# Side jobs of a backward pass in another order, and one filled region dealt unevenly over the DMA engines

## The chip, the cores and the metric

The kernel runs on one core of a Trainium2 chip, in one launch. The metric is the device time of that launch in microseconds (us). Five engines take part: PE (matmul), DVE (vector), ACT (scalar), POOL (GpSimd) and SP (sync). SP and POOL here mostly issue DMAs; all DMAs run on the same 16 DMA engines.

## The reference

One decoder block for a single token, forward and backward, with the gradients of all inputs as outputs. Cut to what matters:

```python
# x: 1x1x448; caches: 8 heads x 32768 x 256; window W = 4096 last positions
def A(x, k_cache, v_cache, wq, wo):
    q = (x @ wq) as 16 heads of 256          # two query heads per cache head
    k, v = last W rows of the caches
    p = softmax(q k^T / 16); o = p v
    return o @ wo
def B(x, w_gate, w_up, w_down):
    return ((x @ w_gate) * (x @ w_up)) @ w_down
h  = x + A(layernorm(x), k_cache, v_cache, wq, wo)
h2 = h + B(layernorm(h), w_gate, w_up, w_down)
out, vjp = jax.vjp(h2 as a function of x, caches, wq, wo, w_gate, w_up, w_down)
return out, *vjp(grad_out)
```

The outputs are out_0 (the block's output), out_1 (gradient of x), out_2 and out_3 (gradients of the K and V caches), out_4 to out_8 (gradients of wq, wo, w_gate, w_up, w_down). The cache gradients have the caches' full shape, 8 x 32768 x 256 in bf16. Only the last 4096 rows of each head depend on anything; the other 28672 rows are zeros and must be written too. That is 14 MB for each of 16 regions (8 heads, two caches), and most of what the kernel moves.

## The kernel before

**Zeros.** A tile `zeros` of 128 x 8192 bf16 is set by one DVE memset. Then SP issues 16 DMAs (line 58), one per head and cache, in the order out_2, out_3 of head 0, then of head 1 and so on. Each writes one region as 896 rows of 16 KB, so 56 rows for each of the 16 DMA engines. SP does nothing else. This is called the fill, and its queue the fill queue; in the profile it is the hardware queue q1.

**Everything else on POOL.** All other transfers are issued by POOL, through the software queue q0: first the rows x and grad_out (lines 88 and 90), then wq (line 92), then the K and V windows, 2 MB each, through eight slots of a tile `S`. POOL issues in program order, so a DMA that waits for something holds back those behind it. Where the program text doesn't force an order, a scheduler chose how the instructions of one engine are interleaved.

**Forward.** For each cache head g: scores, softmax, and moments (lines 308 to 335). Then wo, w_gate and w_up are loaded, the second half of the block is computed, and the gradient comes back to `dh_bc`, `doT` and `dq_bc` (lines 380 to 463).

**Backward, eight stages.** The loop at line 546 has one stage for each cache head g. A stage transposes the head's V window on PE (line 554), forms `dp` (line 559), and builds 32 blocks of the two cache gradients in PSUM (line 588). ACT and DVE in turn copy them (`evac`, lines 208 to 213) into two slots of `S`. The slots alternate by `STG = [5, 6, 7, 0]`, so stage g needs the slots from which stage g-2 was written out. At its end the stage issues two DMAs of 2 MB (line 593, the copy-outs). Three V windows no longer fit and are loaded again during stages 1 to 3 (line 563).

**Side jobs.** After the copy-outs of stage g the text calls the jobs in `side[g]` (line 594). They make the gradients of the weights and the two rows:

- `outer` (line 472) scales a broadcast row on DVE into one of two buffers in `Mt` (`stage_buf`, alternating) and issues the buffer as one DMA. A job must wait until the DMA of two jobs before has landed. o4 to o8 are the five weight gradients.
- `ffn_out` (line 490) loads w_down into the tile `Rt`, makes the block's output row with 14 matmuls and 14 small ones, and writes out_0.
- `dxn_part(i0, i1)` (line 507) loads a part of wq again into `Rt`, and reduces it against `dq_bc` on DVE (line 510). Both parts use the same place in `Rt`. `dx_out` then writes out_1.

Of the kernel before, what the change touches and what calls it, by code (L numbers as in the profile page):

```python
# [7 lines left out]
bf16 = mybir.dt.bfloat16  # L8
# [5 lines left out]
D = 448  # L14
NI = 7
H = 16
G = 8
Dh = 256
W = 4096
# [3 lines left out]
Sk = 32768  # L23
# [5 lines left out]
HQ = H * Dh // 2  # L29
HF = F // 2  # L30
ZW = 8192
# [9 lines left out]
def kernel(  # L41
# [4 lines left out]
    FILL = nc.sync  # L46
    IO = nc.gpsimd

    const = ctx.enter_context(tc.tile_pool(name="const", bufs=1))
    small = ctx.enter_context(tc.tile_pool(name="small", bufs=2))  # L50
    ps = ctx.enter_context(tc.tile_pool(name="ps", bufs=1, space=bass.MemoryType.PSUM))

    zeros = const.tile([128, ZW], bf16)
    V_.memset(zeros[:], 0.0)
    for g in range(G):
        for o in (out_2, out_3):
            reg = o[0, g, 0:Sk - W, :].rearrange("s d -> (s d)").rearrange("(p n f) -> p n f", p=128, f=ZW)
            FILL.dma_start(out=reg, in_=zeros[:].unsqueeze(1).to_broadcast([128, NZ, ZW]))


    S = const.tile([128, NS, SLOT], bf16)
# [21 lines left out]
    def flat_rows(w):  # L83
        return w.rearrange("a b -> (a b)").rearrange("(p x) -> p x", p=128)


    x_bf = const.tile([1, D], bf16, tag="rowa", name="x_bf")
    IO.dma_start(out=x_bf[:], in_=A_x.rearrange("a b d -> (a b) d"))
    go_bf = const.tile([1, D], bf16, tag="rowb", name="go_bf")
    IO.dma_start(out=go_bf[:], in_=grad_out.rearrange("a b d -> (a b) d"))  # L90
    wq_sb = S[:, 1:3, :].rearrange("p a b -> p (a b)")[:, 0:NI * HQ]
    IO.dma_start(out=wq_sb, in_=flat_rows(A_wq))
    load_K(0)
# [58 lines left out]
    def half_to_row(dst, z, bcast, first=True):  # L152

        d3 = dst.rearrange("o (m r) -> o m r", r=NI)
        n = 0
        for i in range(NI):
            for s in range(2):
                lt = z[:, i:i + 1].to_broadcast([128, 128]) if bcast else z[:, i:i + 1]
                P_.matmul(d3[:, :, (7 * s + i) // 2], lhsT=lt, rhs=ident_f[:, s::2],  # L159
                          start=(first and n == 0), stop=(n == 2 * NI - 1), skip_group_check=True)  # L160
                n += 1
# [6 lines left out]
    def layernorm(X, tag):  # L168
        s1 = small.tile([128, 1], f32, tag="ln_s")
        V_.reduce_sum(out=s1[:], in_=X, axis=AX)  # L170
        nm = small.tile([128, 1], f32, tag="ln_nm")
        V_.tensor_scalar(out=nm[:], in0=total(s1[:], 1)[:], scalar1=-1.0 / (2 * D), scalar2=None, op0=ALU.mult)
        xc = small.tile([128, NI], f32, tag="ln_xc")
        V_.tensor_scalar(out=xc[:], in0=X, scalar1=nm[:, 0:1], scalar2=None, op0=ALU.add)
        sq = small.tile([128, NI], f32, tag="ln_sq")
        s2 = small.tile([128, 1], f32, tag="ln_s2")
        V_.tensor_tensor_reduce(out=sq[:], in0=xc[:], in1=xc[:], scale=1.0, scalar=0.0, op0=ALU.mult, op1=ALU.add, accum_out=s2[:])
        rstd = const.tile([128, 1], f32, tag=tag + "rstd")
        S_.activation(out=rstd[:], in_=total(s2[:], 1)[:], func=ACT.Sqrt, bias=eps_t[:, 0:1], scale=1.0 / (2 * D))
        V_.reciprocal(out=rstd[:], in_=rstd[:])  # L180
        xh = const.tile([128, NI], f32, tag=tag + "xh")
        V_.tensor_scalar(out=xh[:], in0=xc[:], scalar1=rstd[:, 0:1], scalar2=None, op0=ALU.mult)
        xb = const.tile([128, NI], bf16, tag=tag + "xb")
        V_.tensor_copy(out=xb[:], in_=xh[:])
        xf = const.tile([128, NI], f32, tag=tag + "xf")
        V_.tensor_copy(out=xf[:], in_=xb[:])
        xx = const.tile([128, NI, 2], bf16, tag=tag + "xx")
        V_.tensor_tensor(out=xx[:], in0=xf[:].unsqueeze(2).to_broadcast([128, NI, 2]), in1=msk[:], op=ALU.mult)
        return rstd, xh, xf, xx
# [30 lines left out]
    rstd1, xh1, xf1, xx1 = layernorm(xX[:], "ln1")  # L220
# [21 lines left out]
    oT_f = const.tile([128, 32], f32)  # L242
    oT_bf = const.tile([128, 32], bf16)
    kbar = const.tile([128, 32], f32)
    dh2_bc = const.tile([128, D], bf16)
# [96 lines left out]
    bc2 = [S[:, 7, NI * HF:NI * HF + F].rearrange("p (i c) -> p i c", i=2), Rt[:, NI * HF:NI * HF + F].rearrange("p (i c) -> p i c", i=2)]  # L342
# [43 lines left out]
    rstd2, xh2, xf2, xx2 = layernorm(hX[:], "ln2")  # L386
# [44 lines left out]
    dh_bc = const.tile([128, D], bf16)  # L431
# [30 lines left out]
    dq_bc = late[:, 0:2 * HQ].rearrange("p (i c) -> p i c", i=2)  # L462
# [4 lines left out]
    def stage_buf():  # L467
        k = 1 + st_ctr[0] % 2
        st_ctr[0] += 1
        return late[:, k * 4096:(k + 1) * 4096]  # L470

    def outer(dst, n0, n1, src, scal, width):

        sb = stage_buf()[:, 0:(n1 - n0) * width].rearrange("p (n c) -> p n c", c=width)
        for n in range(n0, n1):
            V_.tensor_scalar(out=sb[:, n - n0, :], in0=src(n), scalar1=scal[:, n:n + 1], scalar2=None, op0=ALU.mult)
        IO.dma_start(out=dst[:, n0:n1, :], in_=sb)

    o4 = flat_rows(out_4).rearrange("p (i c) -> p i c", i=NI)
    o5 = out_5.rearrange("(b p) n -> p b n", p=128)  # L480
    o6 = flat_rows(out_6).rearrange("p (i c) -> p i c", i=NI)
    o7 = flat_rows(out_7).rearrange("p (i c) -> p i c", i=NI)
    o8 = out_8.rearrange("(c p) n -> p c n", p=128)

    hh = const.tile([128, FC], f32)
# [4 lines left out]
    def ffn_out():  # L490
        wd1 = Rt[:, 0:FC * D].rearrange("p (c n) -> p c n", n=D)
        IO.dma_start(out=wd1, in_=B_w_down.rearrange("(c p) n -> p c n", p=128))
        hX2 = small.tile([128, NI], f32, tag="hX2")
        V_.tensor_scalar(out=hX2[:], in0=hX[:], scalar1=0.5, scalar2=None, op0=ALU.mult)
        t = ps.tile([1, D], f32, tag="tmp", bufs=1)
        for c in range(FC):
            P_.matmul(t[:], lhsT=hh_bf[:, c:c + 1], rhs=wd1[:, c, :], start=(c == 0), stop=False, skip_group_check=True)
        half_to_row(t[:], hX2[:], False, first=False)
        h2 = const.tile([1, D], bf16, tag="rowb", name="h2")
        V_.tensor_copy(out=h2[:], in_=t[:])  # L500
        IO.dma_start(out=out_0.rearrange("a b d -> (a b) d"), in_=h2[:])

    Pq = const.tile([128, NI], f32)
    wq2 = Rt[:, 0:4 * HQ].rearrange("p (i c) -> p i c", c=HQ)
    wq_d = flat_rows(A_wq).rearrange("p (i c) -> p i c", i=NI)

    def dxn_part(i0, i1):
        IO.dma_start(out=wq2[:, 0:i1 - i0, :], in_=wq_d[:, i0:i1, :])
        for i in range(i0, i1):
            V_.tensor_tensor_reduce(out=wq2[:, i - i0, :], in0=wq2[:, i - i0, :], in1=dq_bc[:, i % 2, :], scale=1.0, scalar=0.0,  # L510
                                    op0=ALU.mult, op1=ALU.add, accum_out=Pq[:, i:i + 1])

    def dx_out():
# [4 lines left out]
        V_.tensor_copy(out=dx[:], in_=t[:])  # L518
        IO.dma_start(out=out_1.rearrange("a b d -> (a b) d"), in_=dx[:])

    side = {
        0: [lambda: outer(o6, 0, 4, lambda i: bc2[0][:, i % 2, :], xf2, HF), lambda: outer(o6, 4, 7, lambda i: bc2[0][:, i % 2, :], xf2, HF),
            lambda: outer(o7, 0, 4, lambda i: bc2[1][:, i % 2, :], xf2, HF), lambda: outer(o7, 4, 7, lambda i: bc2[1][:, i % 2, :], xf2, HF)],
        1: [ffn_out] + [lambda b=b: outer(o5, b, b + 8, lambda n: dh_bc[:], oT_f, D) for b in (0, 8)],
        2: [lambda b=b: outer(o5, b, b + 8, lambda n: dh_bc[:], oT_f, D) for b in (16, 24)],
        3: [lambda b=b: outer(o8, b, b + 7, lambda n: dh2_bc[:], hh, D) for b in (0, 7)],
        4: [lambda: dxn_part(0, 4)],
        5: [lambda: dxn_part(4, 7), dx_out],
        6: [lambda i=i: outer(o4, i, min(i + 2, 7), lambda n: dq_bc[:, n % 2, :], xf1, HQ) for i in (0, 2)],
        7: [lambda i=i: outer(o4, i, min(i + 2, 7), lambda n: dq_bc[:, n % 2, :], xf1, HQ) for i in (4, 6)],  # L530
    }


    STG = [5, 6, 7, 0]
# [3 lines left out]
    rowb = late[:, 14336:16384].rearrange("p (k a c) -> p k a c", k=2, a=8)  # L538
# [7 lines left out]
    for g in range(G):  # L546
# [24 lines left out]
        rows = rowb[:, g % 2]  # L571
# [11 lines left out]
        for c in range(T // 2):  # L583
            d_ps = bps.tile([128, 2, 2, Dh], f32, tag="d2", bufs=2)
            for i in range(2):
                t = 2 * c + i
                k, a = t // 8, t % 8
# [38 lines left out]
```

## Time and profile before

| | us |
|---|---|
| median of 3 runs | 818.56 (818.16 to 818.86) |
| the profiled execution, its own time | 818.39 |
| its span, from first to last instruction | 816.6 |
| PE / DVE / ACT busy | 497.6 / 376.8 / 164.9 |

338.66 MB move in this span, at a mean of 415 GB/s. The page's slices are 1/40 of the span each; "DMA" there is the mean busy share of the 16 engines in tenths. In answers about windows the share stands as a number (1.00 is all engines busy), and GB/s beside it. In answers about order of time, the columns are start, duration, engine, line, operation, tiles, count, and in brackets the idle time of that engine just before and what ended it. A DMA's completion adds one count for each of the 16 engines, and the trace holds the time of each count; sorted, these sixteen times tell how far apart the engines are, though not which engine is which.

### The profile page before, as it was taken

What the parts mean: (1) busy time and instruction counts of PE and PEld (TensorE: products, weight loads), DVE (VectorE), ACT (ScalarE), POOL (GpSimd) and SP (SyncE); (2) the same over time, 40 slices, a digit from 0 to 9 for tenths busy, and PEclk for the clock granted to TensorE, in tenths of its full rate; (3) what the DMA queues carried; (4) which work ended last, traced back from release to release, by engine and by line L of the source; (5) the groups of instructions that cost most, each with busy time, mean ns of one, the idle gap of its engine ahead of it and who ended that gap; (6) DMA issues with size and microseconds to landing.
All of it is one profiled execution on the core that took longest, in us unless ns stands there. A gap on an engine that the chain in (4) does not pass through costs nothing.

```text
span 816.6 us, 12117 instructions
## 1 busy us (share of the span) xinstructions
PE 497.6 (61%) x4947; PEld 300.9 (37%) x4991; DVE 376.8 (46%) x1149; ACT 164.9 (20%) x261; POOL 41.7 (5%) x77
## 2 busy tenths in 40 slices
PE   3558869999574946062993468799378940001770
PEld 3545646666343523031981332345124410001110
DVE  4127847667461643028732354565255440404550
ACT  0220201221101000000011233355244420000440
POOL 4000000000000001000000000010010000000000
PEclk9959888999695969565555556555555555555555
DMA  8999999999999999999999999999999999999985
GB/s 322 431 424 429 427 429 426 429 427 426 432 423 426 424 420 418 427 429 432 423 430 427 417 413 426 428 402 429 419 404 426 423 428 400 424 415 432 431 355 237
DMA packets 24632, 338.66 MB, mean 415 GB/s; under 512 B 1312, under 2 KB 1376, under 8 KB 4736
## 3 DMA queue, kind: packets, MB, share of 16 engines
q1 hardware_dynamic: 14592, 234.88, 68.2%
q0 software_dynamic: 9984, 103.00, 30.2%
q8 instruction: 39, 0.64, 0.3%
q14 instruction: 17, 0.14, 0.0%
HBM read 57.28 MB, written 280.59 MB: 414 GB/s over the span
## 4 chain that ended last, share of the span: by engine, by line
issue 50%; DMA 22%; PE 14%; another core or an unknown queue 4%; DVE 4%; POOL 2%; ACT 1%; POOLq 0%; DVEq 0%; ACTq 0%
DMA out_dram<-Mt 9%; DMA out_dram<-S 5%; DMA S<-in_A_wo_dram 4%; PE dq_ps L453 3%; PE d_ps L588 3%; PE tr L554 2%; DMA S<-in_A_v_cache_dram 2%; DMA S<-in_A_wq_dram 2%; PE MT L322 2%; DVE Rt L423 1%; DVE Rt L510 1%; POOL S L75 1%; PE dh_ps L159 1%; DVE S L212 1%
## 5 line engine op out<-in xcount | busy, mean ns | idle before, releaser
L322 PE MATMUL MT<-Rt,S 128*128 128x512 bf16 x468 | 146.7, 391 | 22.5 <-DMA S<-in_A_v_cache_dram 19.8
L588 PE MATMUL d_ps<-R,Mt 32*128 32x512 bf16 x256 | 121.1, 605 | 58.6 <-DVE S L212 57.9
L318 DVE TENSOR_SCALAR Rt<-S,pf 128x256 bf16<-128x256 bf16 x512 | 118.0, 282 | 31.6 <-PE acc L329 16.5
L212 DVE CAST S<-d_ps 128x512 bf16<-128x512 f32 x128 | 87.1, 689 | 63.4 <-ACT S L210 55.6
L210 ACT CAST S<-d_ps 128x512 bf16<-128x512 f32 x128 | 74.9, 586 | 127.7 <-PE d_ps L588 127.7
L266 PE MATMUL tr<-ident_bf,S 128*128 128x128 bf16 x512 | 51.5, 264 | 43.4 <-DMA S<-in_A_k_cache_dram 40.1
L325 PEld LDWEIGHTS <-S 128*128 128x128 bf16 x512 | 50.1, 99 | 62.9 <-issue 7.2
L554 PE MATMUL tr<-ident_bf,S 128*128 128x128 bf16 x512 | 67.6, 304 | 0.7 <-ACT Mt L210 0.7
L588 PEld LDWEIGHTS <-Mt 32*128 32x128 bf16 x256 | 22.8, 113 | 112.8 <-issue 110.8
L329 PE MATMUL acc<-ones_bf,Rt 128*128 128x1 bf16 x1024 | 62.0, 164 | 0.0
L554 PEld LDWEIGHTS <-S 128*128 128x128 bf16 x512 | 48.4, 136 | 24.4 <-issue 24.4
L266 PEld LDWEIGHTS <-S 128*128 128x128 bf16 x512 | 40.5, 120 | 41.9 <-DMA S<-in_A_k_cache_dram 40.6
L325 PE MATMUL acc<-pT_all,S 128*128 128x2 bf16 x512 | 49.3, 166 | 2.6 <-issue 0.9
L165 PE MATMUL t<-st,ones_f 128*128 128x2 f32 x4 | 1.2, 364 | 79.6 <-DVE st L196 79.6
L210 ACT COPY Rt<-tr 128x1024 bf16<-128x1024 bf16 x32 | 32.4, 1012 | 85.1 <-PE tr L266 84.6
L210 ACT COPY Mt<-tr 128x1024 bf16<-128x1024 bf16 x32 | 32.4, 1014 | 60.8 <-PE tr L554 34.3
L329 PEld LDWEIGHTS <-Rt 128*128 128x128 bf16 x1024 | 44.5, 96 | 0.0
L212 DVE COPY Rt<-tr 128x1024 bf16<-128x1024 bf16 x32 | 22.1, 689 | 47.5 <-PE tr L266 46.2
L322 PEld LDWEIGHTS <-S 128*128 128x128 bf16 x512 | 32.2, 97 | 22.3 <-DMA S<-in_A_v_cache_dram 20.0
L331 ACT COPY Mt<-MT 128x512 f32<-128x512 f32 x8 | 4.7, 586 | 165.1 <-remote 73.8
L510 DVE CUSTOM_DVE_ANT_0 Rt<-Rt,Mt 128x2048 bf16<-128x2048 bf16 x7 | 15.6, 2289 | 48.3 <-DMA Rt<-in_A_wq_dram 48.3
L212 DVE COPY Mt<-tr 128x1024 bf16<-128x1024 bf16 x32 | 22.0, 686 | 22.9 <-PE tr L554 15.5
(184 smaller groups left out, 463.5 us busy)
## 6 DMA issues: line engine op xcount, KB each, us to landing
out_dram<-zeros SPq DMA_DIRECT2D x16, 14336.0 KB, 155.7
out_dram<-S POOLq DMA_DIRECT2D x16, 2048.0 KB, 31.0
S<-in_A_v_cache_dram POOLq DMA_DIRECT2D x11, 2048.0 KB, 35.6
S<-in_A_k_cache_dram POOLq DMA_DIRECT2D x8, 2048.0 KB, 27.9
out_dram<-Mt POOLq DMA_DIRECT2D x6, 896.0 KB, 18.2
S<-in_A_wq_dram POOLq DMA_DIRECT2D x1, 3584.0 KB, 15.3
S<-in_A_wo_dram POOLq DMA_DIRECT2D x2, 1792.0 KB, 35.6
out_dram<-Mt POOLq DMA_DIRECT2D x3, 1024.0 KB, 32.5
```

The source lines that it names most:

```text
L75: IO.dma_start(out=dst, in_=cache[0, g, Sk - W:, :].rearrange("(p t) d -> p t d", t=T))
L210: S_.copy(out=out, in_=in_)
L212: V_.tensor_copy(out=out, in_=in_)
L266: P_.transpose(tr[:, i, dh, :], Xw[:, 4 * q + i, dh * 128:(dh + 1) * 128], ident_bf[:])
L318: V_.tensor_scalar(out=pk[:, i, h, :], in0=K[:, t, :], scalar1=pf[:, t, h:h + 1], scalar2=None, op0=ALU.mult)
L322: P_.matmul(MT[:, hf, :], lhsT=Vv[:, t, hf * 128:(hf + 1) * 128], rhs=pk[:, i, :, :].rearrange("p h d -> p (h d)"), start=(t == 0), stop=( ...
L325: P_.matmul(acc[:, 2 * hf:2 * hf + 2], lhsT=Vv[:, t, hf * 128:(hf + 1) * 128], rhs=pT_all[:, g, t, :], start=(t == 0 and hf == 0), stop=(t ...
L329: P_.matmul(acc[:, 4 + 2 * h + dk:5 + 2 * h + dk], lhsT=pk[:, i, h, dk * 128:(dk + 1) * 128], rhs=ones_bf[:, 0:1], start=False, stop=(t == ...
L453: P_.matmul(dq_ps[:, 2 * h + dk:2 * h + dk + 1], lhsT=Mt[:, h // 2, hf, c0:c0 + 128], rhs=doT_f[:, 2 * h + hf:2 * h + hf + 1], start=(hf = ...
L510: V_.tensor_tensor_reduce(out=wq2[:, i - i0, :], in0=wq2[:, i - i0, :], in1=dq_bc[:, i % 2, :], scale=1.0, scalar=0.0, op0=ALU.mult, op1=A ...
L554: P_.transpose(tr[:, i, dh, :], Vw[g][:, 4 * q + i, dh * 128:(dh + 1) * 128], ident_bf[:])
L588: P_.matmul(d_ps[:, i, :, :].rearrange("p w d -> p (w d)"), lhsT=rows[32 * k:32 * k + 32, a, :], rhs=R[32 * k:32 * k + 32, :], start=True, ...
```

## The change

1. The loads of the rows x and grad_out go from POOL to SP, ahead of the fill.
2. The last fill region (out_3, head 7) is written by three DMAs in place of one. Its 896 rows of 16 KB are dealt as 640 rows over 16 engines, 16 rows in pieces of 2 KB over 16 engines, and 240 rows in pieces of 8 KB with an outermost dimension of 15. If the last runs on 15 engines, 15 engines write 57 rows of the region and one writes 41.
3. `dxn_part` loses its load, which becomes `dxn_load`. `ffn_out`, the two o7 jobs and the first wq reload are called ahead of the stages. The two wq parts and `dx_out` move from stages 4 and 5 to stages 0 and 1; o5 moves from stages 1 and 2 to 2 and 3, o8 from 3 to 4, o4 from 6 and 7 to 5 and 6. Stage 7 has no job.

```diff
+    x_bf = const.tile([1, D], bf16, tag="rowa", name="x_bf")
+    FILL.dma_start(out=x_bf[:], in_=A_x.rearrange("a b d -> (a b) d"))
+    go_bf = const.tile([1, D], bf16, tag="rowb", name="go_bf")
+    FILL.dma_start(out=go_bf[:], in_=grad_out.rearrange("a b d -> (a b) d"))
     zeros = const.tile([128, ZW], bf16)
...
+            if g == G - 1 and o is out_3:
+                break
             FILL.dma_start(out=reg, in_=zeros[:].unsqueeze(1).to_broadcast([128, NZ, ZW]))
+    rows = out_3[0, G - 1, 0:Sk - W, :].rearrange("s d -> (s d)").rearrange("(r f) -> r f", f=ZW)
+    FILL.dma_start(out=rows[0:640].rearrange("(p n) f -> p n f", p=128), in_=zeros[:].unsqueeze(1).to_broadcast([128, 5, ZW]))
+    FILL.dma_start(out=rows[640:656].rearrange("r (a c) -> (r a) c", a=8), in_=zeros[:, 0:ZW // 8])
+    FILL.dma_start(out=rows[656:896].rearrange("(e n) (a f) -> e (n a) f", e=15, a=2),
+                   in_=zeros[0:127:9, 0:ZW // 2].unsqueeze(1).to_broadcast([15, 32, ZW // 2]))
...
-    x_bf = const.tile([1, D], bf16, tag="rowa", name="x_bf")
-    IO.dma_start(out=x_bf[:], in_=A_x.rearrange("a b d -> (a b) d"))
-    go_bf = const.tile([1, D], bf16, tag="rowb", name="go_bf")
-    IO.dma_start(out=go_bf[:], in_=grad_out.rearrange("a b d -> (a b) d"))
...
+    def dxn_load(i0, i1):
+        IO.dma_start(out=wq2[:, 0:i1 - i0, :], in_=wq_d[:, i0:i1, :])
+
     def dxn_part(i0, i1):
-        IO.dma_start(out=wq2[:, 0:i1 - i0, :], in_=wq_d[:, i0:i1, :])
...
     side = {
-        0: [o6 0:4, o6 4:7, o7 0:4, o7 4:7],        # each an outer(...), shortened here
-        1: [ffn_out, o5 0:8, o5 8:16],
-        2: [o5 16:24, o5 24:32],
-        3: [o8 0:7, o8 7:14],
-        4: [dxn_part(0, 4)],
-        5: [dxn_part(4, 7), dx_out],
-        6: [o4 0:2, o4 2:4],
-        7: [o4 4:6, o4 6:7],
+        0: [o6 0:4, o6 4:7, dxn_part(0, 4), dxn_load(4, 7)],
+        1: [dxn_part(4, 7), dx_out],
+        2: [o5 0:8, o5 8:16],
+        3: [o5 16:24, o5 24:32],
+        4: [o8 0:7, o8 7:14],
+        5: [o4 0:2, o4 2:4],
+        6: [o4 4:6, o4 6:7],
+        7: [],
     }
+    ffn_out()
+    o7 0:4, o7 4:7
+    dxn_load(0, 4)
```

As the scheduler now deals the instructions out, POOL issues after the loads of the forward pass: w_down, a part of o7, a part of o6, out_0, the rest of o7, the first wq part, the rest of o6, a part of o5, a V window, the second wq part, and only then the copy-outs of stage 0. The last of the o4 jobs stands on DVE within the copies of stage 7, and its DMA on POOL between the copy-outs of stages 6 and 7.

More of the change, by code (lines that the diff above doesn't have):

```diff
@@ L519, in dx_out, with o4_job, o5_job, o67_job @@
         IO.dma_start(out=out_1.rearrange("a b d -> (a b) d"), in_=dx[:])
-    side = {
[L522 to L530, printed above, removed]
-    }
+    def o4_job(i):
+        return lambda: outer(o4, i, min(i + 2, 7), lambda n: dq_bc[:, n % 2, :], xf1, HQ)
+    def o5_job(b):
+        return lambda: outer(o5, b, b + 8, lambda n: dh_bc[:], oT_f, D)
+    def o67_job(w, i0, i1):
+        return lambda: outer((o6, o7)[w], i0, i1, lambda i: bc2[w][:, i % 2, :], xf2, HF)
+    side = {
+        0: [o67_job(0, 0, 4), o67_job(0, 4, 7), lambda: dxn_part(0, 4), lambda: dxn_load(4, 7)],
+        1: [lambda: dxn_part(4, 7), dx_out],
+        2: [o5_job(0), o5_job(8)],
+        3: [o5_job(16), o5_job(24)],
+        4: [lambda b=b: outer(o8, b, b + 7, lambda n: dh2_bc[:], hh, D) for b in (0, 7)],
+        5: [o4_job(0), o4_job(2)],
+        6: [o4_job(4), o4_job(6)],
+        7: [],
+    }
+    ffn_out()
+    o67_job(1, 0, 4)()
+    o67_job(1, 4, 7)()
+    dxn_load(0, 4)
     STG = [5, 6, 7, 0]
```

## Prediction

> **What bounds the kernel now.** I read the page first (DMA by slice, then by queue), then the windows at the end, the timelines of POOL and DVE, and the completion counts of the last DMAs.
>
> ```profile
> DMA  8999999999999999999999999999999999999985
> q1 hardware_dynamic: 14592, 234.88, 68.2%
> q0 software_dynamic: 9984, 103.00, 30.2%
> ```
>
> The DMA engines are busy from the first slice to the last but two, and the fill (q1) is two thirds of that. So an engine's wait elsewhere costs nothing as long as each DMA engine has packets of one queue or the other. What can be won is at the two ends, and in how evenly the 16 engines finish.
>
> ```profile
> 1.31 0.62 POOL L88 DMA_DIRECT2D x_bf<-in_A_x_dram  x1 [0.85 <-POOLq L610]
> 1.93 0.50 POOL L90 DMA_DIRECT2D go_bf<-in_grad_out_dram  x1
> 2.42 0.55 POOL L92 DMA_DIRECT2D S<-in_A_wq_dram  x1
> ```
>
> At the start the first large transfer, wq, is issued behind the two small rows, at 2.42.
>
> ```profile
> 765.00:778.00 13.00, 9.73 (x22) 2.09 (x21) 7.72 (x12) 6.43 (x11) 0.00 (x0) 0.50 1.00 427
> 785.00:790.00 5.00, 3.78 (x9) 0.86 (x9) 2.77 (x4) 2.42 (x5) 0.00 (x0) 0.50 0.97 415
> 790.00:795.00 5.00, 3.83 (x9) 0.90 (x9) 2.77 (x4) 2.40 (x5) 0.00 (x0) 0.50 0.54 229
> 795.00:800.00 5.00, 1.76 (x4) 0.24 (x2) 2.08 (x3) 1.17 (x2) 1.06 (x2) 0.50 0.49 206
> 800.00:805.00 5.00, 0.00 (x0) 0.00 (x0) 0.00 (x0) 0.00 (x0) 0.00 (x0) 0.50 1.00 423
> 805.00:810.00 5.00, 0.00 (x0) 0.00 (x0) 0.00 (x0) 0.00 (x0) 0.00 (x0) 0.50 0.80 341
> ```
>
> The last two numbers are the DMA share and GB/s. Half of the engines idle from 790 to 800, then the last copy-outs run alone. Why those are late:
>
> ```profile
> 675.01 0.69 DVE L212 CAST S<-d_ps 128x512 bf16<-128x512 f32 x1 [0.17 <-ACT S L210]
> 700.63 2.29 DVE L510 CUSTOM_DVE_ANT_0 Rt<-Rt,Mt 128x2048 bf16<-128x2048 bf16 x1 [24.94 <-DMA Rt<-in_A_wq_dram]
> 732.93 2.29 DVE L510 CUSTOM_DVE_ANT_0 Rt<-Rt,Mt 128x2048 bf16<-128x2048 bf16 x1 [23.36 <-DMA Rt<-in_A_wq_dram]
> ...
> 642.91 0.53 POOL L508 DMA_DIRECT2D Rt<-in_A_wq_dram  x1
> 707.65 0.53 POOL L508 DMA_DIRECT2D Rt<-in_A_wq_dram  x1 [31.13 <-DVE Pq L510]
> 778.77 0.54 POOL L593 DMA_DIRECT2D out_dram<-S  x1 [0.17 <-issue]
> 797.73 0.53 POOL L593 DMA_DIRECT2D out_dram<-S  x1 [18.42 <-ACT S L210]
> 798.45 0.53 POOL L593 DMA_DIRECT2D out_dram<-S  x1 [0.19 <-issue]
> ```
>
> DVE sits twice for a wq reload queued behind copy-outs (24.94 and 23.36 us), and the copies of stages 6 and 7 sit behind it on DVE. Stages 0 to 5 issued their copy-outs at 504, 537, 570, 605, 642 and 675, some 34 us apart; those of 6 and 7 come at 778 and 798.
>
> Now the engines. Completion counts in the trace, sorted, of the last fill DMA and of the last copy-out:
>
> ```
> fill, issued 639.96:     777.9 778.1 781.6 781.9 782.0 782.2 782.2 782.5 782.8 785.2 792.4 792.9 797.5 798.3 803.4 805.5
> copy-out, issued 798.45: 809.1 809.1 809.2 809.2 809.2 809.2 809.2 809.2 809.4 809.4 809.5 809.5 810.2 810.5 813.1 814.6
> ```
>
> The slowest engine is still filling at 805.5, when the last copy-out has long been queued: it never idles, and its 814.6 is simply all its work. One engine is late all along (the fill DMA issued at 303.87 ends at 439.7 on it and by 430.3 on the other 15; that of 392.72 at 536.0 against 521.1). The other late ones fell back between 676 and 733, where GB/s drop to 404 and 413. Most engines are different: their second-last pair of copy-outs lands by about 792, the last two (8 packets of 0.611 us each, 4.9 us a DMA) run from 799.4 to 809.2, and 7.5 us in between are idle.
>
> **The change, part by part.** I work against the profiled execution: last landing 814.6, plus 2.0 to the end of the span (816.6), plus 1.8 outside it (818.39). The median, 818.56, is 0.2 above that.
>
> *Start.* wq moves up by the two issues before it, 2.42 - 1.31 = 1.1 us, and with it all later DMA work: -1.1. Bounds: 0 (the rows' reader is no earlier, since DVE's memset runs to 5.14 and the rows landed at 3.1 and 3.6) and -1.6 (both issues and the gap before them). SP issues the two rows in the time in which it waited 5.1 us for the memset; cost nil, and at most 1.1 on the fill, which has wq's packets beside it until its own first packet at 9.65.
>
> *Last fill region.* A 16 KB fill packet takes 0.611 us. 56 of them: 34.2 us per engine. New, on 15 engines: 40 x 0.611 = 24.4; 8 packets of 2 KB, between the rows of 1792 B (0.078) and 2688 B (0.107), taken at 0.085: 0.7; 32 packets of 8 KB at 0.309 (the o4 rows): 9.9. Sum 35.0, +0.8. On the spared engine 25.1, -9.1. Two more SP issues (0.6 us each unless the queue is full) lie under fill already queued.
>
> [...]
>
> *Which engine is late.* The counts show one engine that is late throughout. [...]
>
> *Side jobs.* Bytes and packets stay the same, only their place moves. Per part:
> - The seven reductions of line 510 (2.29 us each, 16 us of DVE) and their two loads leave stage 6's front and enter the copies of stages 0 and 1. Gone: 24.94 + 23.36 of DVE waiting. Added: the first part is issued near 445 and queues behind 7 us of o7, so it lands by about 470, when stage 0's copies start at 475: hidden. The second waits on POOL for the fourth reduction (about 497) and lands some 13 us later; DVE waits for it ahead of the last three copies of stage 0, and behind it on POOL stand the copy-outs of stage 0. Those go from 503.6 to about 520: 9 us of reductions and 7 of waiting.
> - `ffn_out`'s matmuls (14 x 0.58 plus 28 small ones, about 10 us of PE) move from 494-506 to the stretch near 424-440, where PE waited 7.0 once. At worst 10 us more: stage 0 by 520 to 530.
> - o7 ahead of o6 uses the same bytes. o5, o8 and o4 go one stage on; two of them a stage queue 20 us (896-byte rows: 8 blocks are 10 us), beside 20 us of copy-outs, so 34 us a stage rises to at most 40 in stages 2 to 4 and falls after.
> - The last o4 job waits on DVE within stage 7 for its buffer; behind it stand five eighths of stage 7's copies. That buffer's DMA was issued two jobs earlier, with at most 35 us of queue before it, about a stage ago: hidden; 0 to 10 us if not.
>
> So stage 7 issues its last copy-outs at 520 + 7 x 34 = 758 to 530 + 7 x 36 = 782, in place of 798. The fill outlives them and no engine runs dry: the most common engine then has all its work done by 809.2 - 7.5 - 1.1 + 0.8 = 801.4. Cover lasts until 791, about 10 us before that (two copy-outs alone).
>
> *The sum.* What counts is the engine with most work. Spared, if it is the late one: 814.6 - 1.1 - 9.1 = 804.4. The next: 813.1 - 1.1 + 0.8 = 812.8, if the late stretch of 676 to 733 returns as it was. The mean over all engines of (landing minus idle) is 804.8; with the start and the uneven deal 803.9: the floor, if all end together. Between floor and 812.8 I have no row, since that lateness fell in the windows of the wq reloads and those go elsewhere, to times with less in the software queue. I take half of the lateness over 801.4, that is 5.7: last landing 807.1. Span 809.1, time 810.9, by 7.5 us (0.9%) faster.
>
> **The rivals.**
> - *The others stay as late.* For it: engines without idle never catch up. Against: the slow stretches go with transfers that move. 812.8 + 3.8 = 816.6, a gain of 0.2%.
> - *The wrong engine is spared.* Nothing in the profile says which engine the 15 leave out. The late one then keeps its 16 rows and gets another: 814.3 + 3.8 = 818.1, no change. The reordering alone brings nothing, since the slowest engine had no idle time to lose.
> - *Stage 7 comes later, slower than before.* The place: DVE in stages 2 to 6, in order, with copies behind a `Mt` buffer whose DMA stands behind copy-outs (lines like 5.96 and 5.39 us of waiting before line 476 at 656 and 666). The last copy-out takes 10.7 us from issue to landing on a free engine, so it decides from an issue at 791 on and costs time against before from about 805: seven stages of 40.7 us in place of 34. At 42 us a stage the issue is at 814 and the time about 829.
>
> **How the numbers follow.** Differences under 0.2% (1.6 us) can't be told from no change here. The forecast case 0.64, all of it faster; others stay as late 0.14, split 0.08 faster and 0.06 same; wrong engine 0.10 (0.09 same, 0.01 slower); late stage 7 0.12 (0.01 same, 0.11 slower). Faster 0.72, same 0.16, slower 0.12. The range: the floor is 803.9 + 3.8 = 807.7, less what the slow stretches might cost less at their new place (404 and 413 GB/s in place of 429, over 24 and 25 us, are 1.4 and 0.9 us an engine, of which I count three quarters, 1.7), so 806.0; upwards through both "as late" and "wrong engine" to 818.5. Outside lie the late stage 7 and a little below, together under 0.2.
>
> **What would show it.** Right: wq issued near 1.3; no wait of 20 us before line 519 (the old 510); the last copy-outs issued by 785; DMA share 1.00 until about 800; the last completion counts of the fill, not of a copy-out, at the end, within some 6 us of each other. Wrong: one engine's count over 8 us behind the rest (wrong engine), or a window of DMA share near 0.5 ahead of the last copy-outs (late stage 7).

## Result, and the profile after

The changed kernel takes 826.96 us (median; 826.53 to 827.41) against 818.56 before: a ratio of 1.0087, 95% interval 1.006 to 1.0114 (intervals below, in brackets, are of the same kind). It is about 1% slower, where 810.9 was predicted, 0.9% faster. Its profiled execution has a span of 825.1 us and a time of 826.87. The other runs below were each taken beside new runs of the kernel before, whose medians are 818.71 to 819.23 and whose single runs go up to 825.7; a difference is taken against those beside it where nothing else is said.

The page of the changed kernel, DMA by slice, GB/s by slice, and the two large queues:

```profile
DMA  8999999999999999999999999999999999999981
GB/s 343 429 424 430 430 429 426 427 427 429 427 424 428 413 425 420 426 431 431 423 430 428 411 419 430 431 419 425 410 429 427 420 416 421 423 423 428 425 326 37
...
q1 hardware_dynamic: 14979, 234.88, 67.5%
q0 software_dynamic: 9920, 103.00, 29.9%
```

The megabytes are those of before. The last slice carried 237 GB/s before and carries 37 now: for some 20 us almost nothing moves, and yet the kernel has not ended. The side jobs did what they were moved for. POOL's and DVE's timelines (start, duration, engine, line, and in brackets the idle time before with its releaser):

```profile
1.29 0.67 POOL L99 DMA_DIRECT2D S<-in_A_wq_dram  x1 [0.83 <-POOLq L631]
...
513.88 2.29 DVE L519 CUSTOM_DVE_ANT_0 Rt<-Rt,Mt 128x2048 bf16<-128x2048 bf16 x1 [20.18 <-DMA Rt<-in_A_wq_dram]
...
518.76 0.54 POOL L614 DMA_DIRECT2D out_dram<-S  x1 [34.15 <-ACT S L217]
520.62 0.54 POOL L614 DMA_DIRECT2D out_dram<-S  x1 [1.33 <-DVE S L219]
...
762.22 0.53 POOL L614 DMA_DIRECT2D out_dram<-S  x1 [16.40 <-ACT S L217]
762.95 0.53 POOL L614 DMA_DIRECT2D out_dram<-S  x1 [0.19 <-issue]
```

wq goes out at 1.29, stage 0's copy-outs at 519 and 521, the last ones at 762 and 763, 35 us earlier than before. All compute is over by then. The end of the windows (the last two numbers are DMA share and GB/s):

```profile
760.00:780.00 20.00, 1.01 (x2) 0.10 (x1) 1.58 (x3) 0.91 (x2) 1.06 (x2) 0.50 1.00 424
...
785.00:790.00 5.00, 0.00 (x0) 0.00 (x0) 0.00 (x0) 0.00 (x0) 0.00 (x0) 0.50 0.99 399
790.00:795.00 5.00, 0.00 (x0) 0.00 (x0) 0.00 (x0) 0.00 (x0) 0.00 (x0) 0.50 0.93 355
795.00:800.00 5.00, 0.00 (x0) 0.00 (x0) 0.00 (x0) 0.00 (x0) 0.00 (x0) 0.50 0.93 348
800.00:805.00 5.00, 0.00 (x0) 0.00 (x0) 0.00 (x0) 0.00 (x0) 0.00 (x0) 0.50 0.44 159
805.00:810.00 5.00, 0.00 (x0) 0.00 (x0) 0.00 (x0) 0.00 (x0) 0.00 (x0) 0.50 0.25 77
810.00:815.00 5.00, 0.00 (x0) 0.00 (x0) 0.00 (x0) 0.00 (x0) 0.00 (x0) 0.50 0.06 21
...
820.00:825.00 5.00, 0.00 (x0) 0.00 (x0) 0.00 (x0) 0.00 (x0) 0.00 (x0) 0.50 0.04 18
```

Two things are to be read here. From 810 on the share is 0.06, one engine of sixteen (1/16 = 0.0625): one engine ends alone. And from 790 to 800 the share stays at 0.93 while GB/s fall from 424 to 350: engines are busy and move less. The half-idle stretch of before (share 0.49 to 0.54 from 790 to 800) is gone. The completion counts of the three DMAs of the last region, sorted, say the same:

```
640 rows, issued 639.39 (its last three counts): 797.8 798.5 813.2
16 rows in 2 KB, issued 693.91:             784.9 786.0 790.4 790.9 791.0 791.0 791.1 791.5 791.8 792.6 792.7 794.3 796.4 798.8 799.9 814.1
15 pieces, issued 714.40:   747.5 | 800.4 800.7 800.7 800.7 800.8 800.8 801.6 802.4 802.5 803.9 807.7 808.6 809.7 811.5 823.9
```

The third DMA has one count at 747.5, long before its data can have moved and just after SP ended its issue (714.40 + 32.66 = 747.06), and fifteen behind it: it runs on 15 engines. The late engine is one of the fifteen. It ends its packets of 2 KB at 814.1 and then writes 32 packets of 8 KB alone, 9.8 us, until 823.9. The wrong engine was spared.

That explains 0.8 us (one more row of 16 KB on this engine), not 10. The rest is in the packets' durations. Between 797 and 811 the late engine's 16 KB packets take up to 1.27 us in place of 0.611, while one other engine's 8 KB packets take 0.60 to 0.645 in place of 0.309, in step with them. Some of both, with their starts and durations in the trace:

```
late engine, 16 KB:     803.09 1.272   804.37 1.272   805.65 1.272   806.93 1.272   808.20 1.255
another engine, 8 KB:   803.41 0.644   804.06 0.638   804.71 0.644   805.36 0.638   806.01 0.645
```

Both move at half speed; the eleven packets of the late engine from 797 to 810.7 cost it 7 us. In the whole trace 43 of the 480 packets of 8 KB are over 0.5 us.

### The profile page after: what moved, and what is told of

Read it like the earlier page. It is cut to its first block, busy times and chain, and to the rows that moved or that the text cites. A ratio compares the mean times of both kernels' runs of the same rounds, so it can differ in the third digit from the quotient of the medians.

```text
span 825.1 us, 12157 instructions
## 1 busy us (share of the span) xinstructions
PE 508.6 (62%) x4991; PEld 304.1 (37%) x4991; DVE 374.7 (45%) x1149; ACT 165.0 (20%) x261; POOL 40.4 (5%) x75
## 4 chain that ended last, share of the span: by engine, by line
issue 58%; DMA 16%; PE 11%; DVE 4%; POOL 3%; ACT 1%; POOLq 0%; DVEq 0%
DMA S<-in_A_wo_dram 4%; DMA Rt<-in_A_wq_dram 4%; DMA out_dram<-Mt 3%; PE dq_ps L460 3%; DMA S<-in_A_k_cache_dram 3%; DMA S<-in_A_v_cache_dram 2%; PE MT L329 2%; POOL out_dram L484 1%; POOL S L86 1%; DVE Rt L430 1%; POOL out_dram L614 1%; PE dh_ps L166 1%; PE ao L390 1%; PE d_ps L609 1%; PE tr L575 1%
## 5 line engine op out<-in xcount | busy, mean ns | idle before, releaser
L609 PE MATMUL d_ps<-R,Mt 32*128 32x512 bf16 x256 | 124.4, 612 | 92.5 <-DVE S L219 91.8
L329 PE MATMUL MT<-Rt,S 128*128 128x512 bf16 x512 | 157.7, 392 | 20.3 <-DMA S<-in_A_v_cache_dram 19.4
L273 PE MATMUL tr<-ident_bf,S 128*128 128x128 bf16 x512 | 54.1, 273 | 44.2 <-DMA S<-in_A_k_cache_dram 41.0
L332 PEld LDWEIGHTS <-S 128*128 128x128 bf16 x512 | 50.0, 99 | 63.1 <-issue 7.2
L575 PE MATMUL tr<-ident_bf,S 128*128 128x128 bf16 x512 | 68.8, 304 | 3.5 <-ACT Mt L217 3.5
L575 PEld LDWEIGHTS <-S 128*128 128x128 bf16 x512 | 48.5, 135 | 28.0 <-issue 27.8
L273 PEld LDWEIGHTS <-S 128*128 128x128 bf16 x512 | 42.6, 124 | 42.6 <-DMA S<-in_A_k_cache_dram 41.4
L329 PEld LDWEIGHTS <-S 128*128 128x128 bf16 x512 | 32.0, 97 | 21.0 <-DMA S<-in_A_v_cache_dram 20.0
L580 PEld LDWEIGHTS <-Mt 128*128 128x128 bf16 x512 | 20.0, 108 | 36.6 <-DVE Mt L219 13.6
L580 PE MATMUL dp<-doT,Mt 128*128 128x2 bf16 x512 | 22.6, 168 | 12.1 <-DVE Mt L219 10.4
```

Of the source, the lines that this page charges most:

```text
L273: P_.transpose(tr[:, i, dh, :], Xw[:, 4 * q + i, dh * 128:(dh + 1) * 128], ident_bf[:])
L329: P_.matmul(MT[:, hf, :], lhsT=Vv[:, t, hf * 128:(hf + 1) * 128], rhs=pk[:, i, :, :].rearrange("p h d -> p (h d)"), start=(t == 0), stop=( ...
L332: P_.matmul(acc[:, 2 * hf:2 * hf + 2], lhsT=Vv[:, t, hf * 128:(hf + 1) * 128], rhs=pT_all[:, g, t, :], start=(t == 0 and hf == 0), stop=(t ...
L575: P_.transpose(tr[:, i, dh, :], Vw[g][:, 4 * q + i, dh * 128:(dh + 1) * 128], ident_bf[:])
L580: P_.matmul(dp[:, 4 * q + i, :], lhsT=xt[:, i, dh, :], rhs=doT[:, 4 * g + dh:4 * g + dh + 3:2], start=(dh == 0), stop=(dh == 1))
L609: P_.matmul(d_ps[:, i, :, :].rearrange("p w d -> p (w d)"), lhsT=rows[32 * k:32 * k + 32, a, :], rhs=R[32 * k:32 * k + 32, :], start=True, ...
```

## Experiments

The theory: (A) the spared engine is not the late one, and the late engine is halved (1.27 us a packet in place of 0.611) while another engine reads the same part of SBUF, the memory that holds the tiles (a tile's first dimension counts its partitions). Which partitions an engine reads in a transfer over 128 of them, its share, is in no trace; that each engine has such a share, and that the fifteen pieces are read from the shares of others, was my assumption. Rivals are named in each expectation.

**The order alone, and the deal alone.** Four kernels take the change apart. `e1_one_piece` is the changed kernel with the last region as one DMA again. `e2_deal_alone` is the kernel before with only the deal.

```diff
 e1, against the changed kernel
-            if g == G - 1 and o is out_3:
-                break
             FILL.dma_start(out=reg, ...)
-    rows = ...            # and the three DMAs of the deal
 e2, against the kernel before: the same lines added, nothing else
```

> The changed kernel with the last fill region as one DMA of 56 rows an engine again; side jobs and first rows as changed. Theory A (the engine spared is not the late one, and the 8 KB piece makes engines read through each other's share of SBUF and halve): the late engine of the changed kernel had its 40 rows at 813.2, some 7.5 us of that in doubled packets; without them 805.7, plus 16 rows of 0.611 us: last landing 815.5, time 818 to 820, no 16 KB fill packets of 1.2 us in a row after 790. Theory B (the new order of the side jobs itself makes the late engine later, and the deal is innocent): time 825 to 828.

> The kernel before with the last region dealt as 640, 16 and 240 rows; side jobs and first rows as before. Theory A: the late engine keeps its 16 rows and gets another, and its packets double for some 13 of them: 824 to 829. Theory B: the late engine is as before, and the time 817 to 820; if the late engine were the spared one, 809 to 811.

e1 took 816.74 us (816.29 to 817.17), a ratio of 0.9966 [0.9954, 0.9979]. e2 took 828.63 (827.78 to 831.31), 1.0116 [1.0092, 1.014]. So the deal costs 10.2 us with the new order (826.96 - 816.74) and 9.9 with the old (828.63 - 818.71); what it is made of in the old order was not taken apart. In e1 the last two counts are 808.8 and 813.9, no 16 KB packet of the fill after 740 is over 1 us, and the windows end without a fall of GB/s at a full share:

```profile
780.00:790.00 10.00, 0.00 (x0) 0.00 (x0) 0.00 (x0) 0.00 (x0) 0.00 (x0) 0.50 0.99 423
790.00:800.00 10.00, 0.00 (x0) 0.00 (x0) 0.00 (x0) 0.00 (x0) 0.00 (x0) 0.50 0.97 411
800.00:805.00 5.00, 0.00 (x0) 0.00 (x0) 0.00 (x0) 0.00 (x0) 0.00 (x0) 0.50 0.36 154
```

**The rows on SP, and the jobs alone.** `e3_rows_alone` is the kernel before with the loads of x and grad_out on SP. `e6_jobs_alone` is the kernel before with the new lists of side jobs only.

> The kernel before with the loads of x and grad_out on SP, nothing else. By the prediction's first term wq is issued 1.1 us earlier and everything after it: time 817.4. If the start is not on the path of the late engine: 818.5.

> The kernel before with the side jobs as changed; the two rows stay on POOL and the last region is one piece. If the slowest engine had no idle time to lose, as the prediction says, the order alone brings nothing: 817.5 to 819. If it brings all of the 2 us that order and rows together brought: 816.5 to 817.3.

e3: 818.12 us, ratio 0.9997 [0.9981, 1.0013]; no difference. e6: 817.34, 0.9972 [0.9958, 0.9986], 1.5 us below the median of before beside it (818.85). In e6's profile the late engine ends at 814.6, as before, and the next at 808.5. Of the gain, 1.1 us lies behind the last count: from there to the end of the span it is 0.9 us in e6 (815.5 - 814.6), 1.2 in e1 and in the changed kernel, and 2.0 before, where the last DMA was a copy-out.

**Which engine is late.** `e5_probe` is the changed kernel with an even deal and seven very small DMAs behind it, of 2, 4, ... 14 pieces of 1 KB. If a DMA of k pieces runs on the first k engines of a fixed order, in which the engines are numbered here from 0, its last count is late from that k on which takes the late engine in.

```diff
+    for k in range(2, 15, 2):
+        FILL.dma_start(out=flat[at:at + 512 * k].rearrange("(p f) -> p f", p=k), in_=zeros[0:k, 0:512])
+        at += 512 * k
```

> The changed kernel with the last region as one DMA of 768 rows, two even rests before it, and behind it seven tiny DMAs of 2, 4, 6, 8, 10, 12 and 14 pieces of 1 KB. If a DMA of k pieces runs on the k lowest engines, its last completion comes when the latest of these has finished its fill, so the late engine shows as a step of 8 to 15 us between two of them. [...] Time about as that of the run with one piece.

The last counts were 803.5 (k = 2), 807.4 (4), 813.9 (6), 814.1 (8), 814.3, 814.5, 814.7 (14). By that reading the late engine is number 4 or 5, and the engines 0 and 1 are done by 803.5, 2 and 3 by 807.4. The one time taken was 817.66.

**Other source partitions.** `e4_stride4` reads the fifteen pieces from partitions 0, 4, ... 56, and has small DMAs of 4, 5 and 6 pieces behind.

```diff
-                   in_=zeros[0:127:9, 0:ZW // 2]...
+                   in_=zeros[0:57:4, 0:ZW // 2]...
```

> The changed kernel with the 15 source partitions of the 8 KB piece 4 apart (0, 4, ... 56) in place of 9 apart, and 15 of the 16 rows' 128 KB moved into three tiny DMAs of 4, 5 and 6 pieces behind it. [...] Theory A2 (the halving is on the side that is written, or a matter of packet size): no more doubled packets than before, time as the changed kernel. The tiny DMAs: the late engine is number 4 if the last completion steps by 10 us or so between 4 and 5 pieces, number 5 if between 5 and 6.

If the place read from is what halves the engines, I expected 300 to 450 of the 480 packets of 8 KB at about 0.62 us, and a time of 824 to 830. 322 of the 480 are over 0.5 us (43 in the changed kernel), their mean is 0.528 us in place of 0.338, and the windows show engines busy at half the rate:

```profile
795.00:800.00 5.00, 0.00 (x0) 0.00 (x0) 0.00 (x0) 0.00 (x0) 0.00 (x0) 0.50 0.90 201
800.00:805.00 5.00, 0.00 (x0) 0.00 (x0) 0.00 (x0) 0.00 (x0) 0.00 (x0) 0.50 0.87 180
```

Shares of 0.97 and 0.99 went with 411 and 423 GB/s in e1; 0.90 goes with 201 here. Only the source partitions (and 15 KB of small pieces) differ from the changed kernel, so it is the sources that halve the engines, not the size of the packets or the place written to. The small DMAs end at 817.1 (k = 4), 824.0 (5) and 824.2 (6): the late engine is number 4, the fifth. The one time was 826.93, that of the changed kernel, whose late engine ended at 823.9.

**Two tries at reading from the own share.** Both kernels were to have each engine read its 8 KB packets from what I took for its own share; no run shows that these are the shares. The source of such a DMA is written as a start and one constant step in partitions, so both deal a part on SP's queue and a part on POOL's, from a second tile of zeros written in stage 7 and behind a small DMA that was to move POOL's pieces on to other engines. `e7_spare_late` was to give engine 4 about 12 rows of 16 KB fewer than an even share and the other fifteen 0.8 of a row more, with four of the fifteen pieces on SP's queue and eleven on POOL's; `e8_own_share` was to deal as the change does, with eight pieces on SP's queue and seven on POOL's.

```diff
 e8
+    def deal(eng, z, k, p0, n, f):
+        o = flat[at[0]:at[0] + k * n * f].rearrange("(e n f) -> e n f", n=n, f=f)
+        eng.dma_start(out=o, in_=z[p0:p0 + 4 * k - 3:4, 0:f].unsqueeze(1).to_broadcast([k, n, f]))
...
+    deal(FILL, zeros, 8, 0, 32, ZW // 2)
...
+    zb = stage_buf()
+    V_.memset(zb, 0.0)
+    deal(IO, zb, 8, 0, 1, 512)
+    deal(IO, zb, 7, 64, 32, ZW // 2)
```

> [...] Theory A (engine 4 is the one that ends last, and foreign partitions cost the time): no packet of 8 KB over 0.5 us; engine 4 ends near 813.9 - 12 x 0.611 = 806.5, and the end is that of the next engine of the one-piece kernel, 808.8 + 0.8 = 809.6; with 2.0 to the end of the span and 1.8 beyond it 811 to 814. Rival (POOL's queue deals its pieces to the lowest engines again, so engine 4 gets two pieces more instead of none): engine 4 ends at 818 to 826, and the time is 821 to 830. Rival B (any uneven deal costs about 10 us, whoever is spared): 824 to 828.

> [...] Theory A (the 10 us of the deal are engines that halve each other on the same partitions, and the wrong engine is spared): hardly a packet of 8 KB over 0.5 us, no 16 KB packet of the fill over 1 us; the late engine ends at 813.9 + 0.8 = 814.7, and the time is 817.5 to 819.5. Rival B (the uneven deal itself, or its small rows, cost the time): 826 to 828 as in the changed kernel.

e8 took 826.8 us (1.0091 [1.0072, 1.011]), its rival's number, but for another reason. The SP piece's eight counts are 804.7 and then 815.3 815.3 815.9 818.5 820.3 822.7 824.0, and packet by packet seven engines carry 8 KB packets of both queues: POOL's seven pieces fell on seven of the eight engines that had SP's already, the late one among them. It had 16 rows more than planned: 814.7 + 16 x 0.611 = 824.5, measured 824.0. No 8 KB packet of SP's queue was over 0.5 us, but 58 of the 224 of POOL's pieces were, and 35 of the fill's 16 KB packets were over 1 us (775 to 786), where A expected hardly any. POOL's pieces ran on other engines than those for which their partitions were chosen, so this agrees with A, but it does not test it: e8 did not deal as it should have.

e7 took 820.91 (1.0019 [1.0003, 1.0035]), near the lower end of its first rival. Its last count, 817.9, is one of POOL's. 19 packets of 8 KB were over 0.5 us, where A expected none. How POOL's pieces fell there can't be told from the counts, and nothing more is concluded from it.

**One number changed.** `e9_clear4` changes the list of source partitions and leaves all else. In the changed kernel one other engine's packets went in step with the late one's; I took it for a foreign reader in the late engine's share, and chose the steps of 7 so that by the same assumption no other engine reads there.

```diff
-                   in_=zeros[0:127:9, 0:ZW // 2]...
+                   in_=zeros[20:119:7, 0:ZW // 2]...
```

> One number of the change differs: the fifteen pieces are read from partitions 20 to 118 in steps of 7 in place of 0 to 126 in steps of 9. [...] Packets, rows, engines and orders are the same. Theory A (the late engine 4 lost its 9 us to that one foreign reader): the late engine's 16 KB packets take 0.61 us again, it ends at 813.9 + 0.8 = 814.7, and the time is 817.5 to 819.5; other engines may still halve each other and end up to 10 us later than in the one-piece kernel, by 811 to 815. Rival (the small packets, the uneven deal or the place written to cost the time): 826 to 828.

It took 819.5 us (817.32 to 823.86), 0.999 [0.9968, 1.0012]: 7.5 us less than the changed kernel, for another list of source partitions. The completion counts of its last region:

```
640 rows (its last three counts):         794.3 798.2 803.8
16 rows in 2 KB (its last three):         803.4 803.8 804.4
15 pieces (its last four):                812.5 813.2 814.1 816.7
```

The late engine has its 640-row share done at 803.8, over 5 us behind the next (the gap is 5.1 in e1), and its 2 KB packets at 804.4. From there the trace has 32 packets of 8 KB in a row on it, each 0.309 us, and they end with the count of 814.1: 9.8 us ahead of the 823.9 of the changed kernel, and within 0.6 of the 814.7 expected. After 740, two 16 KB packets of the fill are over 1 us, on all engines together, in place of twelve. So the list of source partitions was what cost the late engine its time. That fits A's second half; that it was a reader in the late engine's share is still my assumption. But more packets of 8 KB are slow in all (112 over 0.5 us), on other engines, and one of these now ends last: ten of its 32 packets take 0.596, and its count is the 816.7.

**Sparing engine 4.** `e10_spare_low` uses what e4 and e5 showed: small DMAs of up to four pieces don't wait for the late engine (817.1 with 4 pieces, 824.0 with 5), so engine 4 is relieved by giving rows to 0 to 3. 852 rows go evenly over sixteen engines (53.25 each), 32 rows in four pieces of 8, and 12 rows in two pieces of 6.

```diff
+    FILL.dma_start(out=rows[0:768]..., in_=zeros[:]... [128, 6, ZW])
+    FILL.dma_start(out=rows[768:852]..., in_=zeros[:, 0:84 * ZW // 128])
+    FILL.dma_start(out=rows[852:884]..., in_=zeros[0:13:4, :]... [4, 8, ZW])
+    FILL.dma_start(out=rows[884:896]..., in_=zeros[0:5:4, :]... [2, 6, ZW])
```

> [...] Against an even 56 rows engine 4 gets 2.75 rows fewer: 813.9 - 2.75 x 0.611 = 812.2. Engines 0 and 1 (done by 803.5 in the run with small probes) get 11.25 rows more, 810.4; engines 2 and 3 (by 807.4) 5.25 rows more, 810.6. Theory (engine 4 is the late one and small pieces go to the lowest engines): 812.2 + 2.0 + 1.8 = 816.0 less what the one-piece kernel's 813.9 became in time (816.7 for 813.9, so 1.0 less than the sum): 815.0, range 814.5 to 815.8, below the one-piece kernel's 816.74. Rival (another engine is the late one, or the engines 0 to 3 end later than the probes say): 816.7 to 821.

It took 814.88 us (814.64 to 815.59), 0.9928 [0.99, 0.9956]: 4.4 us less than the kernel before beside it (819.23), and less than any run of e1. The last counts are 811.6 on the even piece (813.9 in e1), 811.4 on the four pieces and 809.1 on the two. The fill is now level to within some 3 us on the engines that end last:

```profile
790.00:800.00 10.00, 0.00 (x0) 0.00 (x0) 0.00 (x0) 0.00 (x0) 0.00 (x0) 0.50 0.87 370
800.00:805.00 5.00, 0.00 (x0) 0.00 (x0) 0.00 (x0) 0.00 (x0) 0.00 (x0) 0.50 0.42 180
805.00:810.00 5.00, 0.00 (x0) 0.00 (x0) 0.00 (x0) 0.00 (x0) 0.00 (x0) 0.50 0.22 96
```

**Is the order worth anything with a good deal?** `e11_low_alone` puts e10's four DMAs into the kernel before; `e12_low_again` is e10 once more, on the same chip.

> The kernel before with the last fill region dealt as in the kernel that spared the low engines (852 rows even, 4 x 8 rows, 2 x 6 rows), and nothing else of the change: side jobs in the old order. If the end is set by engine 4's own work alone, it goes from 814.6 to 814.6 - 1.7 = 812.9, and the time from 818.5 to about 816.8 (others end with the last copy-outs at 809 to 813, the extra rows of engines 0 to 3 fill 7 us in which they idled). If the new order is what makes room for it (engines 0 to 3 can't take the rows beside the late copy-outs), 818 to 820.

> The kernel that spared engine 4 through small pieces to engines 0 to 3, with the new order of side jobs, once more and beside the run with the old order: 814.9 again (814.5 to 815.6). If the two orders are worth the same with this deal, both times agree within 0.2%.

e12: 814.71 us (814.57 to 815.5), 0.9938 [0.9915, 0.9961]. e11: 821.62 (817.45 to 825.02), 1.0024 [1.0003, 1.0045]: 6.9 us more, and 2.8 more than the median of the kernel before beside it (818.81). Both of my expectations were too low. The profile is of an execution of 824.33 us, one of the slowest of the twelve. Its windows and POOL's timeline:

```profile
780.00:790.00 10.00, 7.82 (x18) 1.75 (x17) 5.67 (x9) 4.69 (x8) 0.55 (x1) 0.50 0.46 197
...
805.00:810.00 5.00, 2.45 (x6) 0.44 (x4) 2.77 (x4) 2.15 (x4) 0.80 (x2) 0.50 0.10 43
810.00:815.00 5.00, 0.00 (x0) 0.00 (x0) 0.00 (x0) 0.00 (x0) 0.27 (x1) 0.50 1.00 419
815.00:820.00 5.00, 0.00 (x0) 0.00 (x0) 0.00 (x0) 0.00 (x0) 0.00 (x0) 0.50 0.99 419
```

```profile
809.01 0.53 POOL L600 DMA_DIRECT2D out_dram<-S  x1 [18.41 <-ACT S L217]
809.74 0.53 POOL L600 DMA_DIRECT2D out_dram<-S  x1 [0.19 <-issue]
```

In this execution the fill was done by 805.9, the DMA engines had almost nothing to do from 805 to 809 (share 0.10), and the last two copy-outs ran alone until 820.6. So the end belongs to whichever is later, the fill or the last copy-outs. In the old order the copy-outs can be the later ones; in the new order they are issued by 765, and e1, e6, e10 and e12 each spread by about 1 us (e7 and e9, where 19 and 112 packets of 8 KB are over 0.5 us, by 4.0 and 6.5).

Why the copy-outs come at 809 here and at 798 before is open, but the deal did not delay them in this execution. They are late from stage 0 on, where the first goes out at 512.44 in place of 503.62, and SP issues the first DMA of the last region only at 632:

```profile
503.62 0.54 POOL L593 DMA_DIRECT2D out_dram<-S  x1 [5.27 <-ACT S L210]
```

```profile
512.44 0.55 POOL L600 DMA_DIRECT2D out_dram<-S  x1 [5.76 <-ACT S L217]
```

The first line is of the kernel before, the second of e11. Ten of e11's twelve times are over 820 us, and so are 3 of the 18 of the kernel before beside it; the fastest two of e11 are 817.45 and 817.46, near the 816.8 of the first expectation. That the deal makes the old order slower is therefore not shown; what is shown is that with this deal the new order, with the two rows on SP, is the faster by 6.9 us.

## Why the prediction was wrong

The times of the chain of kernels (medians), with the last count of the late engine:

| Kernel | us | last count |
|---|---|---|
| before | 818.56 | 814.6 |
| new order, one piece (e1) | 816.74 | 813.9 |
| + deal, read in steps of 7 partitions (e9) | 819.5 | 814.1 (another engine: 816.7) |
| + deal as in the change, in steps of 9 | 826.96 | 823.9 |
| new order, deal by the low engines (e10) | 814.88 | 811.6 |

Step by step:

- *Start, -1.1.* The trace shows the shift (wq at 1.29 in place of 2.42), and it is worth nothing that e3 can measure. In e3's profile the last copy-out is even issued later, at 802.13 in place of 798.45: the 800 us in between don't keep a shift of 1.1.
- *Last fill region, +0.8 on 15 engines and -9.1 on one.* The count of 15 engines was right. **The step that failed is the next one: "Spared, if it is the late one".** The late engine is number 4 and had its 32 packets. The prediction called it one late engine and said that nothing in the profile tells which engine is left out; it then gave the wrong one a chance of 0.10. Its rows did not make that so small: a blind deal spares the one late engine of sixteen with a chance of one in sixteen. That the piece runs on 15 engines, and the -9.1 with it, stood on no run; the changed kernel shows the fifteen (one count at 747.5, the others from 800.4 to 823.9), and in place of -9.1 on the late engine the 32 packets that it had too. In these runs the late one is number 4 (k = 4 ends at 817.1, k = 5 at 824.0).
- *The price of the wrong engine, 818.1.* Too low by 8.9. It was "another row", +0.8 on the late engine, for an end at 814.6 - 1.1 + 0.8 = 814.3; e9 confirms that sum, with 814.1 on the late engine. **The term that was put at nothing is the place the packets are read from:** the line of the diff reads `zeros[0:127:9]`, and against e9 it costs the late engine 9.8 us (823.9 - 814.1) and the kernel 7.5 (in e9 another engine, halved too, ends at 816.7). I priced 8 KB packets by the o4 rows (0.309 us), from transfers over 128 partitions. In the changed kernel that is the median of its own 480 packets of 8 KB too, but 43 of them take over 0.5 us.
- *Side jobs.* Right, and in numbers: stage 0's copy-outs at 519 and 521 (520 predicted), the last ones at 762 and 763 (758 to 782 predicted). DVE's second wait is 20.18 us and not the 7 of the working: the second wq part is issued at 484, earlier than the 497 assumed, but lands only by 514, 30 us later and not 13. The sign that I named, no wait of 20 us before line 519, therefore did not come; it cost nothing, since it ends in stage 0 with 240 us to go.
- *"The reordering alone brings nothing."* Nearly so: 1.5 us in e6, 2.0 with the rows in e1. The reason given, that the slowest engine has no idle time to lose, holds: its last count is 814.6 in e6 and 813.9 in e1. Most of e6's gain is in another term, the 2.0 from the last landing to the end of the span, which is 0.9 there.
- *Half of the lateness goes.* In e1 the engine next to the late one ends at 808.8. With the row more that would have been 809.6, against the 807.1 that I took and the 812.8 that I feared. With the right engine spared and no packets doubled the end would have been that one's, 4.3 us ahead of 813.9: about 812.4 by this estimate, in place of 810.9.
- *Late stage 7.* It did not happen. But e11's profile shows the mechanism behind it, copy-outs at the end of the path, in the old order.

The sign that was to show the wrong engine, one count over 8 us behind the rest, is what came: 823.9 against 811.5.

Open: why one engine is late from the third fill on (6 us behind the next at 184 us and 9 at 440 us in the trace of before, 5 at the end of e1), and why the copy-outs of the old order come later in some executions.

## What to carry to other kernels

When a deal of work is to spare one unit, first find out which unit is late, by a probe whose completion depends on it (here DMAs of k small pieces, cheap and clear), and only then write the deal. When packets are handed to chosen DMA engines, look at the partitions they are read from as a part of the price: here 43, 112 or 322 of 480 packets doubled with the list of them, and the sign was a busy share of 0.9 with GB/s down to 350, and to 201 in e4. And two parts can be worth more together than alone: the order alone gave 1.5, the deal by the low engines alone was 2.8 slower at the median (though not shown to be by its own doing), both with the rows on SP gave 4.1 and 4.4, since the end belongs to the later of two chains and the order takes one of them off it.

## What the runs showed of the hardware

- In the changed kernel two DMA engines went at half speed in step with each other: 16 KB packets from 0.611 to 1.27 us, 8 KB ones from 0.309 to 0.60 to 0.645. How many of the 480 packets of 8 KB are over 0.5 us changed with the list of source partitions: 43 with steps of 9, 112 with steps of 7, 322 with steps of 4, there with 201 GB/s at a share of 0.90. That the engines meet at the same part of SBUF is my reading of these counts; no run maps partitions to engines.
- A DMA on SP's queue with 15 pieces has one count at once (747.5, at the end of its issue) and fifteen from 800.4 to 823.9, so it ran on 15 engines. The last counts of small DMAs rise with their pieces (803.5 with 2, 813.9 with 6, 814.7 with 14 in e5), as if they took the engines in a fixed order, and the fifth of that order is the late one (817.1 with 4 pieces, 824.0 with 5 in e4). In e9, with steps of 7, it is not slowed: its 8 KB packets take 0.309 us.
- Pieces on POOL's queue did not go where they were aimed: in e8 seven pieces of that queue fell on seven of the eight engines that SP's queue had used, behind a small piece that was to move them on.
